# Attention with a routed expert layer: the second half's dense tile becomes the fourth tile of its half, and its keys and values are loaded at other times

## The chip, the cores and the metric

The kernel runs on one core of one Trainium2 chip. A core has TensorE (PE, matmuls and transposes), VectorE (DVE), ScalarE (ACT), GpSimd (POOL) and SyncE (SP, which here issues most of the DMAs). The metric is the device time of one execution in microseconds (us), the median of several runs.

## The reference, cut to what matters

Block-sparse attention over 4 batches, 8 heads, 768 tokens and 24 blocks of 32, then a layer of 8 experts that picks one expert for every token.

```python
mask = np.abs(blk_i - blk_j) <= 1
mask = mask | (blk_i == 0) | (blk_j == 0) | (blk_i == n_blocks - 1) | (blk_j == n_blocks - 1)
for qb in range(n_blocks):
    for kb in sampled_blocks[qb]:                      # 3 sampled blocks
        mask[qb * block:(qb + 1) * block, kb * block:(kb + 1) * block] = True
attn = softmax(np.where(mask, scale * q @ k.T, -1e9))
x = (attn @ v).transpose(0, 2, 1, 3).reshape(B * S, H * D)      # 3072 x 512
logits = x @ w_gate + modality_bias[modality_id]
e_idx = np.argmax(logits, axis=1)
for e in range(E):
    h = np.maximum(x[mask] @ w1[e], 0.0)               # mask = e_idx == e
    out[mask] = gate_w[mask, None] * (h @ w2[e])
```

The first and the last block of queries see all keys ("dense"); the other 22 see a window, the first and the last block and three sampled ones ("sparse").

## The kernel before

The batches are worked off in two halves of two. A half has 12 tiles of 128 tokens (2 batches x 2 blocks x 32): one dense tile (blocks 23 and 0) and 11 sparse ones. The work of a tile is cut into items: a dense tile has eight (`("d", b, pr)`, batch and pair of heads), a sparse tile four (`("s", half, m, n, b)`). The list `items` holds the eight dense items of the first half, then all 88 sparse ones; after the sparse items whose numbers are in `DENSE_AFTER` two dense items of the second half are put in each time.

The loop at the end of attention runs over steps t. In a step, each stage of an item runs `LAG` steps after its first: S scores (L401 dense, L557 sparse), M maxima, X exponentials (L423, L573), T transposes (L433, L582), A copies, W weighted sums (L451 dense, L604 sparse, at lag 7 for dense and 5 for sparse), V the own sampled values (L613, lag 7), O division (L460, L470), Y transposes of the output, G gate. An item's S thus runs at the step that is its index in `items`. Scores are computed for two items at once, at every second step. The order of instructions on every engine is that in which the code is written; each engine works off its own in this order.

Loads hang on steps (`side`). For every sparse tile SyncE issues a query (L146, followed by a load of block numbers into registers, L536), value rows that the tile needs anew (L511 to L517; a half's first two tiles need more of them) and six sampled "own" value blocks (L545), the latter two after the V stage of the tile two before has released their buffer. GpSimd copies a tile's keys together out of the dense keys, which stay in SBUF (`share_k`, L484, L488, L502), and hands on value rows (`share_v`, L527). The dense keys and values of the second half (batches 2 and 3, 1.5 MB each for keys and for values) come in six pieces of 256 KB each (L159 keys, L165 values), every second step from the steps in `DENSE_IN`: values, first half of the keys, second half of the keys. `KD_SLOT` and `VD_SLOT` say which slots of SBUF they take.

A finished tile has a number tau in the order of tokens; two tiles with tau and tau ^ 1 are routed together (`routing`: argmax of the gate, ranks in the expert, L353 and what follows), as "fillers" between the stages. When 16 and 18 tiles are ranked, `choose` picks the experts of the first two groups of 256 tokens, and `rows_of` turns the positions of a group's tokens into the rows to gather (`g_`) and the rows of the output (`s_`); it is called a third time for all other groups. Expert groups gather tokens, split weights into a high and a low part (L752, L755) and run both layers (L810 to L812, L825 to L827); the first two start before attention ends.

Of the kernel before, what the change touches and what calls it, by code (L numbers as in the profile page):

```python
# [15 lines left out]
ALU = mybir.AluOpType  # L16
# [4 lines left out]
P = 128  # L21
B, H, S, D = 4, 8, 768, 64
BLK = 32
# [6 lines left out]
NT = NTOK // P  # L30
# [27 lines left out]
DENSE_DVE = ((0, 0), (0, 1))  # L58
DENSE_AFTER = (21, 29, 45, 47)
LAG = {'d': {'S': 0, 'M': 1, 'X': 2, 'T': 4, 'A': 4, 'W': 7, 'O': 8, 'V': 101, 'Y': 11, 'G': 13}, 's': {'S': 0, 'M': 1, 'X': 2, 'T': 4, 'A': 4, 'W': 5, 'V': 7, 'O': 8, 'Y': 10, 'G': 13}}  # L60
# [13 lines left out]

DENSE_IN = ((19, 14, 30), (49, 38, 44))
Q_IN = 22
# [14 lines left out]
def attention_moe(ctx, tc, kD, qD, qH, v0, v1, blocks, modality, w_gate, bias, w1, w2, out):  # L91
    nc = tc.nc
# [29 lines left out]
    with ExitStack() as actx:  # L122
# [13 lines left out]
        kd, vd = {}, {}  # L136
        KD_SLOT, VD_SLOT = (0, 1, 2, 9), (2, 3, 3, 3)
        ad = slot(4)
# [496 lines left out]
        lgs = {}  # L635

        rank_ends = {4: 0, 8: 4, 12: 8, 14: 12, 16: 14, 18: 16, 20: 18, 22: 20, 24: 22}
        fillers = []
# [416 lines left out]
        def rows_of(tp, n, g_, s_, hold=None):  # L1055
            i_, f_ = ((lambda name, dt=dt: small.tile([P, NCOL], dt, name=name, bufs=1)[:, 0:n]) for dt in (I32, F32))
            pad, tf, to = f_("pad"), f_("tf"), f_("to")
            tk, tb, tn = i_("tk"), i_("tb"), i_("tn")
            nc.vector.tensor_scalar(to, tp[:, 0:n], 0.5, float(NTOK // 2 - 1), ALU.is_lt, ALU.add)
            yield  # L1060
            nc.vector.tensor_tensor(g_, tp[:, 0:n], to, ALU.add)
            if hold is not None:
                ready[NEAR] = True
                while not hold:
                    yield
            yield
            nc.vector.tensor_scalar(pad, tp[:, 0:n], 0.0, 8192.0, ALU.is_equal, ALU.mult)
            nc.vector.tensor_scalar(tk, g_, 7, None, ALU.logical_shift_right)
            yield
            nc.vector.tensor_scalar(tn, g_, 5, 1, ALU.logical_shift_right, ALU.bitwise_and)  # L1070
            nc.vector.tensor_scalar(tf, tk, float(NB // 2), float(-NB // 2), ALU.is_ge, ALU.mult)
            yield
            nc.vector.tensor_scalar(tb, g_, 6, 1, ALU.logical_shift_right, ALU.bitwise_and)
            nc.vector.tensor_tensor(tf, tf, tk, ALU.add)
            yield
            nc.vector.scalar_tensor_tensor(pad, tb, float(S - 2 * BLK), pad, ALU.mult, ALU.add)
            nc.vector.tensor_tensor(to, tf, tn, ALU.add)
            yield
            nc.vector.tensor_scalar(to, to, 0.5, float(S), ALU.is_le, ALU.mult)
            yield  # L1080
            nc.vector.scalar_tensor_tensor(to, tf, float(-2 * BLK), to, ALU.mult, ALU.add)
            yield
            nc.vector.scalar_tensor_tensor(to, g_, float(-BLK), to, ALU.add, ALU.add)
            yield
            nc.vector.tensor_tensor(s_, to, pad, ALU.add)
# [144 lines left out]
        xrs, turns, banks, sums, ats, gated, written = {}, {}, {}, {}, {}, set(), {}  # L1230
# [5 lines left out]
        def tau_of(m, half):  # L1236
            return half * (NT // 2) + m + 1

        def end_tile(m, half):
            tau = tau_of(m, half)  # L1240
            gate(tau, turns.pop((m, half)))
            gated.add(tau)
            if tau ^ 1 in gated:
                t = tau - tau % 2
                fillers.append(routing(t, lgs.pop(t), [xrs.pop((t % (NT // 2) + n - 1, half)) for n in range(2)]))

# [72 lines left out]
        for g in range(2 * NM):  # L1319
            half, m = divmod(g, NM)  # L1320
            t = at["s", half, m, 0, 0]
# [89 lines left out]
        with man:  # L1411
            constants()
            for token in START:
# [3 lines left out]
                elif op == "h":  # L1417
                    t = int(token[1:])
# [90 lines left out]
```

## Time and profile before

| | us |
|---|---|
| median of 3 runs (530.39, 526.32, 525.06) | 526.32 |
| the profiled execution | 523.66 |
| its span | 521.9 |
| PE busy in the span | 499.5 |
| DVE busy | 388.4 |
| ACT busy | 335.5 |
| POOL busy | 244.9 |

Attention fills the span to some 225 us, with the first two expert groups starting in its last part; the other groups follow. Busy times are those of one execution; a busy PE is not PE at its peak.

### The profile page before, as it was taken

The page shows a single profiled execution, that of the slowest core. Times are in us where ns is not written, and L with a number is a line of the kernel's source. Part 1 is how long each engine was busy: PE and PEld are TensorE (multiplying, and loading weights), DVE is VectorE, ACT ScalarE, POOL GpSimd, SP SyncE. Part 2 cuts the span into 40 slices and gives each one's busy share as a digit, 9 for nine tenths or more (in the row PEclk, how much of TensorE's full clock was granted, in tenths as well). Part 3 has the DMA queues.
Part 4 walks back from the last instruction along what each step waited for, and adds up shares of the span by engine and source line. Part 5 has one row for each costly group of instructions (what it writes and reads, how often), then busy time and mean ns, then how long its engine had stood idle before and what let it go on. Part 6 is the DMA issues. An engine that isn't in the chain of part 4 may idle for free.

```text
span 521.9 us, 18958 instructions
## 1 busy us (share of the span) xinstructions
PE 499.5 (96%) x7124; PEld 420.6 (81%) x7124; DVE 388.4 (74%) x1136; ACT 335.5 (64%) x765; POOL 244.9 (47%) x514
## 2 busy tenths in 40 slices
PE   7999999989899999899999999999999999999995
PEld 5667776767778777688989798998989899898974
DVE  5886688686689899967986868667686766768573
ACT  3799787978789978844545655555565545655561
POOL 6779685576458884312275051323324222241423
PEclk9999999999999999999999999999999999999999
DMA  8997885999756778965878797879669696877860
GB/s 293 332 249 227 241 222 184 244 228 258 196 174 191 207 219 245 273 192 200 242 281 294 246 297 258 266 233 301 200 240 284 227 295 202 280 223 251 260 209 25
DMA packets 59063, 123.84 MB, mean 237 GB/s; under 512 B 9681, under 2 KB 17618, under 8 KB 58962
## 3 DMA queue, kind: packets, MB, share of 16 engines
q1 hardware_dynamic: 54704, 108.88, 68.7%
q0 software_dynamic: 4256, 13.65, 7.9%
q8 instruction: 58, 0.95, 0.8%
q14 instruction: 43, 0.35, 0.3%
q10 hardware_dynamic: 2, 0.00, 0.0%
HBM read 105.97 MB, written 12.86 MB: 228 GB/s over the span
## 4 chain that ended last, share of the span: by engine, by line
PE 73%; DMA 11%; DVE 7%; ACT 3%; SPq 2%; issue 2%; POOL 0%; DVEq 0%; POOLq 0%; ACTq 0%
PE bank L810 8%; PE bank L812 8%; PE bank L811 8%; PE bank L827 7%; PE bank L826 7%; PE bank L825 7%; PE bank L557 6%; PE bank L582 6%; DMA slot<-x_d,gi 5%; PE bank L604 3%; PE bank L613 3%; PE bank L451 2%; DMA slot<-w 2%; PE bank L630 2%; PE bank L401 2%
## 5 line engine op out<-in xcount | busy, mean ns | idle before, releaser
L755 DVE TENSOR_TENSOR slot<-slot 128x1024 fp32r<-128x1024 f32 x99 | 124.6, 1272 | 63.1 <-ACT slot L752 54.9
L752 ACT CAST slot<-slot 128x1024 fp32r<-128x1024 f32 x104 | 107.0, 1047 | 68.3 <-PE bank L811 49.5
L810 PE MATMUL bank<-slot 128*128 128x256 f32 x384 | 108.4, 282 | 0.2 <-issue 0.2
L812 PE MATMUL bank<-slot 128*128 128x256 f32 x384 | 107.9, 281 | 0.1
L811 PE MATMUL bank<-slot 128*128 128x256 f32 x384 | 107.6, 280 | 0.0
L573 ACT ACTIVATE a<-y,mn 128x256 f32<-128x256 f32 x176 | 88.7, 511 | 7.9 <-DVE mn L565 7.7
L846 POOL DMA_INDIRECT out<-slot,si x20 | 27.3, 1364 | 109.5 <-ACT slot L842 106.5
L827 PE MATMUL bank<-slot 128*128 128x512 f32 x192 | 75.9, 395 | 0.4 <-DVE slot L818 0.4
L826 PE MATMUL bank<-slot 128*128 128x512 f32 x192 | 75.9, 395 | 0.0
L825 PE MATMUL bank<-slot 128*128 128x512 f32 x192 | 75.8, 395 | 0.0
L810 PEld LDWEIGHTS bank<-slot 128*128 128x128 f32 x384 | 72.3, 188 | 0.6
L811 PEld LDWEIGHTS bank<-slot 128*128 128x128 f32 x384 | 72.2, 188 | 0.6
L812 PEld LDWEIGHTS bank<-slot 128*128 128x128 f32 x384 | 72.2, 188 | 0.3 <-DVE slot L755 0.3
L565 DVE CUSTOM_DVE_ANT_1 y<-bank,smask 128x256 f32<-128x256 f32 x176 | 66.2, 416 | 0.5 <-PE bank L557 0.3
L502 POOL COPY slot<-slot 128x128 f32 x264 | 63.6, 293 | 0.0
L527 POOL TENSOR_SCALAR slot<-slot 32x1024 f32<-32x1024 f32 x40 | 41.7, 1042 | 33.2 <-issue 12.8
L587 ACT COPY at<-bank 128x512 f32<-128x512 f32 x88 | 50.6, 576 | 9.0 <-PE bank L582 9.0
L582 PE MATMUL bank<-ident,a 128*128 128x128 f32 x352 | 52.1, 280 | 3.0 <-issue 2.2
L557 PE MATMUL bank<-slot,q_raw 64*32 64x256 f32 x1408 | 48.7, 382 | 0.0
L582 PEld LDWEIGHTS bank<-ident,a 128*128 128x128 f32 x352 | 38.1, 141 | 7.3 <-issue 2.3
L827 PEld LDWEIGHTS bank<-slot 128*128 128x128 f32 x192 | 36.1, 188 | 9.2 <-DVE slot L818 0.9
L826 PEld LDWEIGHTS bank<-slot 128*128 128x128 f32 x192 | 36.0, 188 | 8.3 <-DVE slot L755 0.4
(307 smaller groups left out, 859.8 us busy)
## 6 DMA issues: line engine op xcount, KB each, us to landing
slot<-w SPq DMA_DIRECT2D x100, 512.0 KB, 5.2
slot<-v SPq DMA_DIRECT2D x180, 128.0 KB, 4.0
x_d<-xr SPq DMA_DIRECT2D x22, 256.5 KB, 4.2
q_raw<-qH SPq DMA_DIRECT2D x22, 256.0 KB, 4.8
slot<-v SPq DMA_DIRECT2D x16, 256.0 KB, 5.1
slot<-slot SPq DMA_DIRECT2D x120, 32.0 KB, 4.4
slot<-kD SPq DMA_DIRECT2D x13, 256.0 KB, 3.6
slot<-v SPq DMA_DIRECT2D x4, 768.0 KB, 12.4
```

What stands on the lines that cost most here:

```text
L557: nc.tensor.matmul(sp[u][32 * pr:32 * pr + 32, b * 256:(b + 1) * 256], lhsT=q[r, b * NPAIR + pr, n, :], rhs=kv[r, s0:s0 + 8, b, pr, :], st ...
L565: nc.vector.tensor_tensor_reduce(y[:, u, :].rearrange("p (s f) -> p s f", s=8), sp[u][:, b * 256:(b + 1) * 256].rearrange("p (s f) -> p s ...
L573: nc.scalar.activation(a[:, u, :], y[:, u, :], AF.Exp, bias=mn[:, u:u + 1], scale=-1.0, accum_out=total[:, u:u + 1])
L582: nc.tensor.transpose(tp[:, k:k + P], a[:, u, c * P:(c + 1) * P], ident)
L752: nc.scalar.copy(h, s)
L755: (eng or (nc.gpsimd if n in POOL_SPLITS else nc.vector)).tensor_tensor(l, s, h.bitcast(F32), ALU.subtract)
L810: nc.tensor.matmul(o, lhsT=h[:, fs], rhs=xh[g % 2][:, c, :], start=c == 0 and f % 2 == 0, stop=False)
L811: nc.tensor.matmul(o, lhsT=h[:, fs], rhs=xl[g % 2][:, c, :], start=False, stop=False)
L812: nc.tensor.matmul(o, lhsT=l[:, fs], rhs=xh[g % 2][:, c, :], start=False, stop=c == 3 and f % 2 == 1)
L825: nc.tensor.matmul(o, lhsT=hh[0][:, f, ts_], rhs=h[:, fs], start=f == 0, stop=False)
L826: nc.tensor.matmul(o, lhsT=hh[0][:, f, ts_], rhs=l[:, fs], start=False, stop=False)
L827: nc.tensor.matmul(o, lhsT=hl[f // 4][:, f % 4, ts_], rhs=h[:, fs], start=False, stop=f == 7)
```

## The change

The dense tile of the second half gets tau 15 instead of 12, the place behind three sparse tiles (`DENSE_PLACE`). Its items go into the list later (`DENSE_AFTER`), its keys earlier and its values later (`DENSE_IN`), and the values of batch 3 go into slot 0 instead of slot 3. `rows_of` takes the new place into account with seven more instructions on VectorE and one `yield` more in each of its three calls. The modality table, which is ordered by tau, is reordered on the host.

```diff
-DENSE_AFTER = (21, 29, 45, 47)
+DENSE_AFTER = (35, 41, 51, 53)
+DENSE_PLACE = (0, 3)
-DENSE_IN = ((19, 14, 30), (49, 38, 44))
+DENSE_IN = ((38, 14, 20), (57, 26, 32))
-        KD_SLOT, VD_SLOT = (0, 1, 2, 9), (2, 3, 3, 3)
+        KD_SLOT, VD_SLOT = (0, 1, 2, 9), (2, 3, 3, 0)
...
             nc.vector.tensor_tensor(tf, tf, tk, ALU.add)
             yield
+            d, first = DENSE_PLACE[1], NT // 2
+            nc.vector.tensor_scalar(dj, tk, float(first), None, ALU.is_ge)
+            yield
+            nc.vector.tensor_scalar(to, tk, float(first + d), float(-d - 1), ALU.is_ge, ALU.mult)
+            nc.vector.tensor_tensor(dj, dj, to, ALU.add)
+            nc.vector.tensor_scalar(to, tk, float(first + d + 1), float(d), ALU.is_ge, ALU.mult)
+            nc.vector.tensor_tensor(dj, dj, to, ALU.add)
             nc.vector.scalar_tensor_tensor(pad, tb, float(S - 2 * BLK), pad, ALU.mult, ALU.add)
             nc.vector.tensor_tensor(to, tf, tn, ALU.add)
+            nc.vector.tensor_tensor(to, to, dj, ALU.add)
             yield
             nc.vector.tensor_scalar(to, to, 0.5, float(S), ALU.is_le, ALU.mult)
             yield
             nc.vector.scalar_tensor_tensor(to, tf, float(-2 * BLK), to, ALU.mult, ALU.add)
+            nc.vector.scalar_tensor_tensor(to, dj, float(2 * BLK), to, ALU.mult, ALU.add)
...
         def tau_of(m, half):
-            return half * (NT // 2) + m + 1
+            return half * (NT // 2) + (DENSE_PLACE[half] if m < 0 else m + (m >= DENSE_PLACE[half]))
+
+        def tile_of(tau):
+            half, n = divmod(tau, NT // 2)
+            return (-1 if n == DENSE_PLACE[half] else n - (n > DENSE_PLACE[half])), half
...
-                fillers.append(routing(t, lgs.pop(t), [xrs.pop((t % (NT // 2) + n - 1, half)) for n in range(2)]))
+                fillers.append(routing(t, lgs.pop(t), [xrs.pop(tile_of(t + n)) for n in range(2)]))
...
-                1, 3, 4, 0, 2)).reshape(P, NT),
+                1, 3, 4, 0, 2).reshape(P, NT)[:, order]),
```

From the table follow these steps. Dense items start at 30, 40, 58 and 62 before, and at 44, 52, 64 and 68 now. Keys of batch 2: 14 to 18 and 30 to 34 before, 14 to 24 now; keys of batch 3: 38 to 48 before, 26 to 36 now. Values of batch 2: 19 to 29 before, 38 to 48 now; of batch 3: 49 to 59 before, 57 to 67 now.

The first place is SyncE's queue at the value loads of the second half's first tile (before, the fifth piece of batch 3's values, an output row, that tile's value rows L511 to L514, a query, the sixth piece):

```order
L165 DMA slot<-v 128x512
L1297 DMA x_d<-xr 128x513
L511 DMA slot<-v 32x1024 x2
L513 DMA slot<-v 32x2x1024
L514 DMA slot<-v 32x2x1024
L146 DMA q_raw<-qH 128x512
L536 TENSOR_LOAD rb_i
L165 DMA slot<-v 128x512
```

After the change (line numbers one higher and more), the same queue at the value rows of the half's second tile, L512 to L518; ahead of this stand the rows of the first tile, the first piece and six own values:

```order
L166 DMA slot<-v 128x512
L147 DMA q_raw<-qH 128x512
L537 TENSOR_LOAD rb_i
L166 DMA slot<-v 128x512
L1311 DMA x_d<-xr 128x513 x2
L512 DMA slot<-v 32x1024 x2
L517 DMA slot<-v 32x1024
L518 DMA slot<-v 32x1024
L166 DMA slot<-v 128x512
```

The six pieces, which before ended at the first tile's value rows, now begin behind them and stand around those of the second tile.

The second place is TensorE where the second half's dense items begin. Before, the scores of its last four come with two sparse items of the half's first tile between them:

```order
L401 MATMUL bank<-slot,qd 64x512 x4
L401 MATMUL bank<-slot,qd 64x256 x4
L597 MATMUL bank<-rexp,fold 32x8 x4
L613 MATMUL bank<-slot,at 32x64 x32
L582 MATMUL bank<-ident,a 128x128 x8
L557 MATMUL bank<-slot,q_raw 32x256 x16
L630 MATMUL bank<-wg_raw,xT 64x8 x8
L604 MATMUL bank<-slot,at 64x64 x16
L582 MATMUL bank<-ident,a 128x128 x4
L620 MATMUL bank<-ident,xr 128x128 x4
L433 MATMUL bank<-ident,a 128x128 x6
L401 MATMUL bank<-slot,qd 64x512 x4
```

Now (L402 dense scores, L558 sparse scores, L434 dense transposes), two tiles further on:

```order
L402 MATMUL bank<-slot,qd 64x512 x4
L402 MATMUL bank<-slot,qd 64x256 x4
L605 MATMUL bank<-slot,at 64x64 x16
L583 MATMUL bank<-ident,a 128x128 x4
L621 MATMUL bank<-ident,xr 128x128 x4
L583 MATMUL bank<-ident,a 128x128 x4
L558 MATMUL bank<-slot,q_raw 32x256 x16
L598 MATMUL bank<-rexp,fold 32x8 x4
L614 MATMUL bank<-slot,at 32x64 x32
L583 MATMUL bank<-ident,a 128x128 x4
L434 MATMUL bank<-ident,a 128x128 x6
L402 MATMUL bank<-slot,qd 64x512 x4
```

The pairs keep their distance of two sparse items and lie beside the same kinds of work, after the half's second tile instead of within its first.

The third place is VectorE in the first call of `rows_of` (before: `to` is the index of the output row, L390 and L565 belong to ranks and attention):

```order
L390 TENSOR_SCALAR lhs<-iota_f,rlo,code 128x128
L1079 TENSOR_SCALAR to<-to 128x2
L1081 SCALAR_TENSOR_TENSOR to<-tf,to 128x2
L458 TENSOR_SCALAR rt<-bank 128x8
L459 RECIPROCAL rt<-rt 128x8
L460 TENSOR_TENSOR xr<-bank,rt 128x512
```

After the change:

```order
L391 TENSOR_SCALAR lhs<-iota_f,rlo,code 128x128
L1080 TENSOR_SCALAR to<-tk 128x2
L1081 TENSOR_TENSOR dj<-dj,to 128x2
L1082 TENSOR_SCALAR to<-tk 128x2
L1083 TENSOR_TENSOR dj<-dj,to 128x2
L1084 SCALAR_TENSOR_TENSOR pad<-tb,pad 128x2
L1085 TENSOR_TENSOR to<-tf,tn 128x2
L1086 TENSOR_TENSOR to<-to,dj 128x2
L1088 TENSOR_SCALAR to<-to 128x2
L459 TENSOR_SCALAR rt<-bank 128x8
L460 RECIPROCAL rt<-rt 128x8
L461 TENSOR_TENSOR xr<-bank,rt 128x512
```

Eight short rows instead of two stand ahead of the division of a tile (L459 to L461).

## Rows read from the trace of the kernel before

**Rows 1.** The page, part 1: busy us, share of the span, instructions.
```profile
PE 499.5 (96%) x7124; PEld 420.6 (81%) x7124; DVE 388.4 (74%) x1136; ACT 335.5 (64%) x765; POOL 244.9 (47%) x514
```

**Rows 2.** Windows of 20 us: length, busy us of each engine, PE clock, DMA share, GB/s.
```profile
40.00:60.00 20.00, 18.88 (x516) 14.50 (x506) 13.56 (x63) 17.40 (x58) 15.66 (x39) 1.00 0.77 227
60.00:80.00 20.00, 19.16 (x466) 14.51 (x464) 15.21 (x70) 16.45 (x54) 15.49 (x47) 1.00 0.84 235
80.00:100.00 20.00, 19.09 (x481) 14.53 (x476) 15.45 (x70) 16.60 (x56) 10.88 (x27) 1.00 0.73 208
100.00:120.00 20.00, 17.45 (x491) 13.78 (x476) 15.37 (x76) 15.22 (x52) 14.64 (x42) 1.00 0.91 237
120.00:140.00 20.00, 18.22 (x423) 13.33 (x423) 13.14 (x56) 16.86 (x54) 7.74 (x25) 1.00 0.94 239
140.00:160.00 20.00, 20.00 (x548) 15.81 (x546) 15.25 (x80) 15.53 (x53) 13.60 (x43) 1.00 0.54 161
...
260.00:280.00 20.00, 20.00 (x125) 17.77 (x125) 18.32 (x36) 10.86 (x14) 11.34 (x8) 1.00 0.81 282
```

**Rows 3.** Timeline of PE, 30 to 200 us: start, us, line, [idle before <- releaser].
```profile
52.36 0.45 PE L604 MATMUL bank<-slot,at 128*64 128x64 f32 x8 [0.81 <-issue]
...
65.48 1.09 PE L557 MATMUL bank<-slot,q_raw 64*32 64x256 f32 x32
...
70.30 1.09 PE L557 MATMUL bank<-slot,q_raw 64*32 64x256 f32 x32
...
71.41 1.23 PE L613 MATMUL bank<-slot,at 128*32 128x64 f32 x64
...
77.21 0.92 PE L451 MATMUL bank<-slot 128*64 128x64 f32 x24 [0.52 <-DVE mn L565]
...
115.47 1.09 PE L582 MATMUL bank<-ident,a 128*128 128x128 f32 x8 [2.18 <-issue]
...
131.40 0.33 PE L433 MATMUL bank<-ident,a 128*128 128x128 f32 x1
133.20 0.70 PE L433 MATMUL bank<-ident,a 128*128 128x128 f32 x5 [1.48 <-issue]
```

**Rows 4.** Timeline of DVE, 109 to 118 us.
```profile
111.95 1.03 DVE L381 CAST rhi<-r 128x4 f32<-128x4 int32 x1
...
114.55 0.69 DVE L460 TENSOR_TENSOR xr<-bank,rt 128x512 f32<-128x512 f32 x1
```

**Rows 5.** Timeline of POOL, 22 to 170 us.
```profile
106.84 2.15 POOL L488 TENSOR_SCALAR slot<-slot 128x256 f32<-128x256 f32 x5 [2.13 <-DMA slot<-kD]
...
111.91 4.40 POOL L527 TENSOR_SCALAR slot<-slot 32x1024 f32<-32x1024 f32 x4
```

**Rows 6.** Windows of 5 us, columns as in rows 2.
```profile
115.00:120.00 5.00, 4.54 (x97) 3.77 (x98) 4.45 (x21) 3.29 (x11) 4.75 (x14) 1.00 1.02 267
...
130.00:135.00 5.00, 3.52 (x115) 2.81 (x114) 3.72 (x10) 3.23 (x11) 2.08 (x2) 1.00 1.01 249
...
200.00:205.00 5.00, 5.00 (x147) 3.60 (x149) 4.80 (x28) 4.58 (x13) 0.42 (x2) 1.00 0.88 259
```

**Rows 7.** Timeline of SP: DMA issues, start, us in the issue.
```profile
96.12 0.86 SPq L146 DMA_DIRECT2D q_raw<-qH  x1
98.49 1.33 SPq L545 DMA_DIRECT2D slot<-v  x3
...
105.91 0.33 SPq L165 DMA_DIRECT2D slot<-v  x1
...
127.33 0.35 SPq L165 DMA_DIRECT2D slot<-v  x1
```

**Rows 8.** DMA issues, 118 to 140 us: count, KB each, median us to landing.
```profile
slot<-v SPq DMA_DIRECT2D x4, 256.0 KB, 6.3
```

**Rows 9.** Two lines of `rows_of`: count, ns min/median/max, first and last start, forms.
```profile
L1059 DVE TENSOR_SCALAR to<-bank x3: 146/156/190, 197.6 to 263.2; 128x2 f32<-128x2 f32 x2, 128x38 f32<-128x38 f32 x1
L1070 DVE TENSOR_SCALAR tn<-gi_e x2: 161/586/1012, 199.2 to 225.3; 128x2 int32<-128x2 int32 x2
```

More of the change, by code (lines that the diff above doesn't have):

```diff
@@ L1056, in rows_of @@
             i_, f_ = ((lambda name, dt=dt: small.tile([P, NCOL], dt, name=name, bufs=1)[:, 0:n]) for dt in (I32, F32))
-            pad, tf, to = f_("pad"), f_("tf"), f_("to")
+            pad, tf, to, dj = f_("pad"), f_("tf"), f_("to"), f_("dj")
             tk, tb, tn = i_("tk"), i_("tb"), i_("tn")
@@ L1486 @@
     k, q = cols(inputs["k"]), cols(inputs["q"])
+    order = [h * (NT // 2) + n for h, d in enumerate(DENSE_PLACE) for n in (*range(1, d + 1), 0, *range(d + 1, NT // 2))]
     arrays = {
```

## The prediction

> **What bounds the kernel now.** I began with the page's busy shares. TensorE is busy 96% of the span [rows 1], so whatever a new order can give back must come out of the 4% in which it waits. The windows of 20 us show where that is in the stretch that the change touches, steps 19 to 72 of the schedule, some 40 to 150 us: from 40 to 140 us TensorE is idle for 1.12, 0.84, 0.91, 2.55 and 1.78 us, 7.20 together [rows 2]. From 140 us to 160 it has no gap, nor has it among the expert groups, the last two rows there [rows 2]. No work of TensorE is removed, so 7.20 us, 1.4% of the span, is the most that a better order here can return.
>
> Then the single waits on TensorE's timeline, four of which hold 4.99 us of the 7.20 [rows 3]. They are of three kinds. At 115.47 it had waited 2.18 us until a transpose could take its PSUM bank: the division of an earlier tile (L460 on VectorE) ended at 115.24 [rows 4], 0.23 us before, and in the program that transpose does wait for VectorE. VectorE was late: a cast of 128x4 took 1.03 us while GpSimd ran four 32x1024 copies back to back for 4.40 us [rows 4, 5], which had piled up behind key copies that waited 2.13 us for a dense key transfer [rows 5]. At 52.36 and 133.20 (0.81 and 1.48 us) TensorE stopped inside a run: of six transposes one started at 131.40 and the other five from 133.20 [rows 3], and the second of them waits for nothing in the program. I take these to be instructions that arrived late, since the queues are full then: DMA share 1.02 at 115 to 120 us and 1.01 at 130 to 135 [rows 6]. At 77.21 (0.52 us) it waits for VectorE behind a pair of dense items.
>
> **The change part by part.** *The order of items.* Nothing is added on TensorE, ScalarE or GpSimd in the attention. The four dense pairs start at steps 44, 52, 64 and 68 instead of 30, 40, 58 and 62. Both routings concerned, of the tile pairs (12, 13) and (14, 15), still become ready at steps 76 and 84, because the last item that each waits for comes as late as before. So from step 84 on all keeps its order, except for the VectorE rows below. The wait behind a dense pair moves with it: 0, with bounds of 0.52 either way.
>
> *The 2.18 us wait.* The last dense keys were issued at step 48, six steps before the key copies that need them; now it is step 36, eighteen before. That takes away GpSimd's wait of 2.13 us, and the two sets of value copies that ran back to back there get these key copies between them (two other sets now stand together, at steps 38 and 42). I count 2.0 of the 2.18 as gained; bounds 0, since VectorE can be late for a bank elsewhere, and 2.18.
>
> *Late instructions.* These waits depend on when a fetch falls into full queues. Four of the six dense value pieces that left in 105 to 122 us go behind that stretch, but there they meet others. I take 0.5 of the 2.29 (0.81 + 1.48) as gained; bounds 2.29 gained and 1.48 lost, one more such wait. The Trainium skill (Runtime: NRT & Kernel Launch, Instruction fetch mechanics) calls the refill of an engine's instructions mostly hidden. By that page these would be ordinary waits that a new order may remove; the gain would be 2.29 and the sum below 1.8 us better. The five transposes that start late without a wait in the program speak against it.
>
> *Values of the third dense batch.* Their last piece was issued at step 29 and needed at step 37; now it is issued at 48 and needed at 51. What there is to spend: from the scores of step 32 (65.48) to the first weighted sum of step 37 (77.21) it is 11.7 us [rows 3], and steps 46 to 51 are built alike; the piece is the sixth of six blocks, some 0.7 us later, so 12.4. What is spent: SyncE is held until the sums of step 46 release a buffer, 2.3 us after that step's scores (70.30 to 71.41 + 1.23 at step 34 [rows 3]); then come two value issues at 0.4 each, a query and a register load (2.37 us from 96.12 to 98.49), three own values (1.33) and its own issue of 0.4 [rows 7]: 7.2 us. A 256 KB value took 6.3 us to land in the busiest stretch [rows 8]: 13.5, so 1.1 us late there, and on time where it lands in 5. I take 0.5; bounds 0 and 2.4 (another set of own values of 1.33 ahead of it).
>
> *Values of the fourth batch.* They went out from 105.91 to 127.33 us [rows 7]; now eight steps later, beside the first loads of the half's first two tiles, which carry more value rows than others, and are needed at step 71. The last piece follows only two values behind the release of step 66: 2.3 + 0.8 + 0.4 + 6.3 = 9.8 us, and the same lead of 12.4 covers it. What is dear is the stretch: four of the six pieces move into it, 4 x 0.262 MB at 249 GB/s [rows 6] is 4.2 us, the upper bound; the queues have room behind it (share 0.54 at 140 to 160 us [rows 2]), the lower bound is 0, and I take 0.3. The Trainium skill (SBUF — State Buffer, Summary: rules for kernel authors) reckons with about 358 GB/s between HBM and SBUF. By that page the queues would not be full at 249, and the 0.3 us would be nothing; the share of 1.01 at 249 GB/s says that they are full.
>
> *Seven more VectorE rows in each of three calls* that turn gathered indices into output rows. Such a row takes 0.15 to 0.16 us undisturbed, and one took 1.01 [rows 9], like the cast beside GpSimd's copies. Two calls lie at 197.6 to 231 us: 14 x 0.155 = 2.2 us. VectorE is busy 4.80 of 5 us there, but TensorE 5.00 [rows 6], so matmuls cover most of it; if that cover is gone, the 2.2 us stand on the path, and 1.7 more if two rows meet a GpSimd copy (0.86 each). I take 0.4; bounds 0 and 3.9. The call has one more step, which makes the second group's choice half a step later; its gather keeps its place among GpSimd's rows: 0. The third call starts at 263.2 us [rows 9], where TensorE is busy 20.00 of 20 [rows 2]: 0, hidden by expert matmuls, and 1.1 if they did not hide it. The slot that now takes the fourth batch's values is last read by key copies issued at step 48, nine steps before the first load: no wait, 0.
>
> Sum: -2.0 - 0.5 + 0 + 0.5 + 0.3 + 0.4 = -1.3 us. The profiled execution took 523.66 us (span 521.9), 2.66 under the median of 526.32, and would come to 522.4; from the median I forecast **525.0 us**.
>
> **The rivals.** *The waits only change place.* VectorE, ScalarE and GpSimd run close behind TensorE in attention; a bank that is free in one place is late in another. For it: the idle time is spread over all five windows. Against it: the largest wait has a chain of its own with the dense keys at its head. Time: 526.3, give or take 1.5.
>
> *All waits of the stretch go.* For it: 140 to 160 us, half empty now, takes over transfers from a full stretch. The gain is 7.20 less the 1.2 of costs, so 520.3. Against it: 2.21 of the 7.20 lies in small waits that no load explains.
>
> *Slower: the fourth batch's values collide with the first tiles of the half.* SyncE then has six pieces, eight value issues of two tiles, twelve own values and two queries in eleven steps. Place: the weighted sum of step 71. It decides once the last piece is issued later than 6.1 us after the scores of step 66 (12.4 less 6.3 to land). Price: the 4.2 us without room, plus one more late fetch of 1.48 while the share stays at 1, and nothing gained: 532.0. Against it: the queues are half empty from 140 us on.
>
> *Slower by the VectorE rows:* 3.9 us on the path less the 2.0 gained, 528.2. It decides where VectorE, at 96%, has no slack left.
>
> **How the numbers follow.** The forecast, a gain of 0 to 4.5 us, gets 0.45; the waits that change place 0.22; all waits gone 0.17; the collision 0.12; the VectorE rows 0.04. A measurement of this kernel can hardly tell less than 1%, 5.3 us, from no change (three runs lay from 525.06 to 530.39). Under 521.1 lies only the case with all waits gone: faster 0.17. Over 531.6 lies only the collision: slower 0.12. Within 1%: 0.71. The range leaves out the collision and a part of the all-gone case (0.2 together), and takes in the VectorE case with the spread of the first rival: 519.5 to 530.0.
>
> **What would show it.** Right: no wait of TensorE over 1 us at the half's first tile; key copies there with no wait for dense keys; DMA share at 140 to 160 us up from 0.54; rows of the new seven near 0.15 us each; the first expert matmuls about 1 us earlier. Wrong: a wait of TensorE at the weighted sums of step 51 or 71 for a value transfer; SyncE issuing value pieces two steps or more behind TensorE; or a gap after 180 us that outweighs it all. I would be most wrong if the stretch from 180 to 240 us, whose order I leave as it is, depended on the phase in which attention reaches it.

## The result, and the profile after

The changed kernel takes 532.29 us (median of six runs, 528.33 to 535.54) against 525.06 for the kernel before (six runs, 523.36 to 530.39): a ratio of 1.0123, 95% interval 1.0086 to 1.016. A second set of runs gave 1.0115 (1.0068 to 1.0162). So it is slower by some 6 us, outside the range given; a gain of 1.3 us was forecast. Executions in which the chip itself ran some per cent slow are left out of all ratios here, and a profile taken of one is not read.

The profiled execution is the slowest of its six (535.54 us, span 533.8), and that has to be kept in mind while reading it. The page's first part, as in [rows 1]:

```profile
PE 507.0 (95%) x7124; PEld 425.0 (80%) x7124; DVE 390.8 (73%) x1157; ACT 336.4 (63%) x765; POOL 247.9 (46%) x514
```

The count of matmuls is the same; VectorE has its 21 rows more. TensorE's busy time has risen by 7.5 us with the same work. The windows of 20 us, columns as in [rows 2]:

```profile
40.00:60.00 20.00, 19.71 (x511) 15.74 (x512) 14.13 (x70) 18.10 (x60) 17.88 (x50) 1.00 0.68 206
60.00:80.00 20.00, 18.59 (x530) 14.22 (x528) 13.63 (x66) 16.44 (x55) 13.08 (x35) 1.00 0.87 247
80.00:100.00 20.00, 18.52 (x436) 13.06 (x434) 12.72 (x56) 14.90 (x47) 13.06 (x35) 1.00 0.86 229
100.00:120.00 20.00, 15.46 (x304) 11.26 (x300) 11.56 (x59) 10.99 (x36) 8.87 (x22) 0.83 0.78 219
120.00:140.00 20.00, 20.00 (x521) 15.53 (x514) 15.28 (x74) 18.36 (x62) 12.48 (x37) 1.00 0.60 176
140.00:160.00 20.00, 19.63 (x450) 14.92 (x458) 15.34 (x64) 16.38 (x52) 11.36 (x32) 1.00 0.87 231
...
220.00:240.00 20.00, 15.37 (x326) 13.84 (x325) 11.71 (x68) 9.67 (x21) 6.40 (x7) 0.83 0.50 140
```

From 120 to 140 us TensorE has no gap now (1.78 us before), and the queues' share has moved from there (0.94 to 0.60) to 140 to 160 us (0.54 to 0.87), as forecast. But two windows are worse than any of before, and in both the granted clock is 0.83. TensorE's timeline says what stands there (line numbers are one higher than before, ten higher behind `rows_of`):

```profile
105.86 0.80 PE L452 MATMUL bank<-slot 128*64 128x64 f32 x20
111.20 0.48 PE L452 MATMUL bank<-slot 128*64 128x64 f32 x4 [4.54 <-DMA slot<-v]
...
112.66 2.84 PE L402 MATMUL bank<-slot,qd 64*64 64x512 f32 x16
...
116.30 1.30 PE L452 MATMUL bank<-slot 128*64 128x64 f32 x24
...
137.36 1.52 PE L402 MATMUL bank<-slot,qd 64*64 64x512 f32 x16
...
227.41 0.78 PE L605 MATMUL bank<-slot,at 128*64 128x64 f32 x20
232.11 0.91 PE L605 MATMUL bank<-slot,at 128*64 128x64 f32 x12 [3.92 <-issue]
```

The first is the weighted sum of step 51: twenty of its 24 matmuls run, then TensorE waits 4.54 us for the sixth block of the third dense batch's values. The second is in the middle of a run of 32 matmuls that wait for nothing in the program; in the kernel before the same run was broken in the same part, for 1.12 us. Behind each of them TensorE runs at its lower level for a while, which the windows of 5 us show:

```profile
110.00:115.00 5.00, 3.80 (x24) 1.82 (x24) 1.96 (x11) 1.68 (x5) 0.00 (x0) 0.54 0.92 233
115.00:120.00 5.00, 5.00 (x92) 3.82 (x84) 2.79 (x11) 1.56 (x3) 0.00 (x0) 0.78 0.46 146
...
230.00:235.00 5.00, 2.89 (x22) 2.77 (x22) 0.23 (x1) 0.63 (x2) 0.00 (x0) 0.50 0.29 103
235.00:240.00 5.00, 5.00 (x109) 4.42 (x108) 4.63 (x31) 3.13 (x5) 1.61 (x2) 0.83 0.07 12
```

Sixteen dense scores take 2.84 us there and 1.52 at 137.36; the 24 matmuls of a weighted sum take 1.30 instead of 0.92 [rows 3]. Between the two profiled executions lie 11.9 us. The two waits make 4.54 + 3.92 - 1.12 = 7.3 of them, and the four windows lack 2.30 + 1.10 + 2.50 + 0.85 = 6.8 us of full clock, at most, since TensorE stood still for a part of them; the vanished waits of 2.18 and 1.48 us [rows 3] go off that. By steps: the scores of step 96 start 5.4 us later than before (201.90 against 196.53), those of step 102 6.9 us later, and the other 5.0 us come behind them.

Why the piece came late stands on SyncE's timeline and on the chain of waits:

```profile
97.06 0.42 SPq L166 DMA_DIRECT2D slot<-v  x1
97.79 1.42 SPq L546 DMA_DIRECT2D slot<-v  x3
99.38 1.24 SPq L166 DMA_DIRECT2D slot<-v  x1
...
102.53 0.35 SPq L147 DMA_DIRECT2D q_raw<-qH  x1
104.40 1.33 SPq L546 DMA_DIRECT2D slot<-v  x3
105.78 0.41 SPq L166 DMA_DIRECT2D slot<-v  x1
```

```profile
105.78 5.38 DMA slot<-v
111.16 0.04 issue
111.20 0.48 PE bank L452 x4
```

The piece left at 105.78, when the sum that needs it had almost begun (105.86). It landed in 5.38 us. What is late is the issue.

### The profile page after: what moved, and what is told of

Read it like the earlier page. It is cut to its first block, busy times and chain, and to the rows that moved or that the text cites. A ratio compares the mean times of both kernels' runs of the same rounds, so it can differ in the third digit from the quotient of the medians.

```text
span 533.8 us, 18974 instructions
## 1 busy us (share of the span) xinstructions
PE 507.0 (95%) x7124; PEld 425.0 (80%) x7124; DVE 390.8 (73%) x1157; ACT 336.4 (63%) x765; POOL 247.9 (46%) x514
## 4 chain that ended last, share of the span: by engine, by line
PE 60%; DVE 15%; DMA 13%; issue 4%; SPq 3%; ACT 3%; POOL 1%; POOLq 0%; DVEq 0%; ACTq 0%
PE bank L811 7%; PE bank L813 7%; PE bank L812 6%; PE bank L827 6%; PE bank L828 6%; PE bank L826 6%; PE bank L558 5%; DMA slot<-x_d,gi 4%; PE bank L583 4%; DMA slot<-v 3%; DVE y L566 3%; PE bank L614 2%; PE bank L605 2%; PE bank L452 2%; DMA slot<-w 2%
## 5 line engine op out<-in xcount | busy, mean ns | idle before, releaser
L756 DVE TENSOR_TENSOR slot<-slot 128x1024 fp32r<-128x1024 f32 x99 | 120.9, 1235 | 60.3 <-ACT slot L753 49.0
L558 PE MATMUL bank<-slot,q_raw 64*32 64x256 f32 x1408 | 50.8, 382 | 0.9 <-issue 0.9
```

What stands on the lines that cost most here:

```text
L558: nc.tensor.matmul(sp[u][32 * pr:32 * pr + 32, b * 256:(b + 1) * 256], lhsT=q[r, b * NPAIR + pr, n, :], rhs=kv[r, s0:s0 + 8, b, pr, :], st ...
L756: (eng or (nc.gpsimd if n in POOL_SPLITS else nc.vector)).tensor_tensor(l, s, h.bitcast(F32), ALU.subtract)
```

## The experiments

Ratios are to the kernel before, run beside the kernel on the same chip, with 95% intervals. "Steps 96 to 102" is read from TensorE's timeline, from the first scores of step 96 to the first of step 102; from there on all orders hold the same matmuls. (The expectations count to the last matmul of scores, 0.7 us more.)

| kernel | ratio | interval | steps 96 to 102, us |
|---|---|---|---|
| before | 1 | | 12.3 |
| changed; again | 1.0123; 1.0115 | 1.0086 to 1.0160; 1.0068 to 1.0162 | 13.8; 14.2 |
| values 3rd batch at 34 to 44 | 1.0067 | 1.0030 to 1.0104 | 14.4 |
| at 39 to 49 | 1.0171 | 1.0112 to 1.0231 | 13.3 |
| at 19 to 29 | 1.0152 | 1.0100 to 1.0205 | 13.8 |
| keys 4th batch at 38 to 48 | 1.0133 | 1.0081 to 1.0186 | 14.1 |
| without the seven rows; again | 1.0078; 1.0079 | 1.0045 to 1.0111; 1.0046 to 1.0113 | 12.0; 12.2 |
| seven rows alone | 1.0040 | 1.0005 to 1.0074 | 13.4 |
| fourteen rows alone | 1.0112 | 1.0058 to 1.0167 | 17.3 |
| five rows on GpSimd | 1.0175 | 1.0125 to 1.0226 | 15.8 |
| new order, old load steps | 1.0104 | 1.0046 to 1.0161 | 15.7 |
| the same without the rows | 1.0046 | 1.0012 to 1.0080 | 12.7 |
| half the new order, no rows | 1.0058 | 1.0019 to 1.0098 | 12.5 |
| changed, rows behind attention; again | 1.0134; 1.0095 | 1.0074 to 1.0194; 1.0058 to 1.0132 | 12.0; not read |
| order and old loads, rows behind | 1.0075 | 1.0042 to 1.0108 | 13.2 |
| before, rows behind; again | 0.9984; 1.0009 | 0.9951 to 1.0017; 0.9970 to 1.0048 | not read; 12.1 |

**The changed kernel again.** No edit.

> The changed kernel once more, beside the runs of the kernel before on one chip, to see which of its waits come back. Theory A (one late piece): the wait at the weighted sum of step 51 is there again, 3 to 5.5 us, with half clock behind it; the time is 1.0 to 1.4% over the kernel before. Theory B (the wait at 228 us, a late fetch of instructions): the wait there comes back at the same matmul, 0.5 to 4 us long, so that its size is chance and the mean loss by it is 1 to 2 us. If the 3.92 us belong to the change, it is over 3 us again.

Its span is 529.2 us, without either of the large waits. TensorE's timeline:

```profile
100.08 0.55 PE L583 MATMUL bank<-ident,a 128*128 128x128 f32 x3 [2.03 <-issue]
...
109.84 0.80 PE L452 MATMUL bank<-slot 128*64 128x64 f32 x20
111.16 0.34 PE L452 MATMUL bank<-slot 128*64 128x64 f32 x4 [0.52 <-DMA slot<-v]
...
210.89 0.64 PE L631 MATMUL bank<-wg_raw,xT 128*64 128x8 f32 x16 [1.67 <-DVE rt L459]
...
227.72 0.57 PE L605 MATMUL bank<-slot,at 128*64 128x64 f32 x12 [0.82 <-issue]
```

and SyncE's:

```profile
105.75 0.43 SPq L166 DMA_DIRECT2D slot<-v  x1
```

The last piece left at the same time, to 0.03 us, and the matmuls that need the block start at the same time (111.16 and 111.20). TensorE only reached them 4 us later, because it had lost those before; 2.03 of them stand at 100.08, inside a run of four transposes. So in these two executions the wait is what is left of a fixed arrival; and since the time over the kernel before is the same, theory A, that one late piece makes the loss, falls with this run. In this profile the scores of step 96 start 4.1 us later than in the kernel before, those of step 102 6.0 us, and only 1.3 us come behind them. The wait at 228 us is 0.82 here, as theory B has it: its size is chance, its place is not.

**When the values are loaded.** One row each (39 and 19 stand for 34 in two more; the last moves the keys of the fourth batch):

```diff
-DENSE_IN = ((38, 14, 20), (57, 26, 32))
+DENSE_IN = ((34, 14, 20), (57, 26, 32))
+DENSE_IN = ((38, 14, 20), (57, 38, 44))
```

> The values of the third dense batch are asked for at steps 34 to 44 instead of 38 to 48, all else as in the changed kernel. Theory A (the late last piece makes the loss): the 4.54 us wait of TensorE at the weighted sum of step 51 and the half clock in the 6.8 us behind it go; 532.3 less 4.5 and some 2.6 is 525.2 us, between 524 and 527. Theory B (the loss lies after 180 us, in a stretch that depends on the phase in which attention reaches it, above all the 3.92 us wait at 228 us): the wait at step 51 goes, but the time stays at 529 or more, or moves by the phase either way. Theory C (the 21 VectorE rows cost it): 529 or more, with the 3.92 us wait still there.

> The values of the third dense batch are asked for one step later still, at steps 39 to 49, all else as in the changed kernel. A step takes some 2.1 us there. Theory A: the wait at the weighted sum of step 51 grows from 4.5 to between 5.6 and 6.8 us, and the time from 532.3 to between 533 and 535. Theory B: the phase behind the wait shifts by 1 to 2 us; the time may go either way by 2 us and the wait at 228 us changes or goes. Theory C: no change, 532.3.

> The changed kernel with the third dense batch's values alone back at the steps of the kernel before, 19 to 29; the keys stay at 14 to 36, the fourth batch's values at 57 to 67. Theory D: the waits for values between 60 and 115 us go, last scores at 208 to 211 us, 0 to 0.4% over the kernel before. Rival O: last scores at 214 us or later, 0.8% or more over. Rival K (what counts is the mass in a stretch, and 20 pieces between 42 and 82 us now fill that one): waits of 2 us or more in 40 to 85 us instead, 0.5 to 1% over.

> The changed kernel with the fourth dense batch's keys at steps 38 to 48, as in the kernel before, and no longer at 26 to 36; the values of the third batch stay at 38 to 48. Theory A: what decides is the last piece's issue, which is as late as before or later by the key issues beside it: a wait of 4.5 to 7 us at the weighted sum of step 51, 1.2 to 1.8% over the kernel before. Theory D: two pieces at each even step, 3.1 MB in the full stretch, so waits for own values beside that one, 1.6 to 2.5% over. If only the count of pieces ahead of step 38 mattered: 1% or less over.

Four steps earlier the wait at step 51 is gone, but in the profile smaller ones stand where it was full, for own values that came behind the dense pieces:

```profile
89.58 1.09 PE L614 MATMUL bank<-slot,at 128*32 128x64 f32 x62 [1.26 <-DMA slot<-v]
...
99.90 1.09 PE L614 MATMUL bank<-slot,at 128*32 128x64 f32 x62 [0.83 <-DMA slot<-v]
...
108.51 1.09 PE L614 MATMUL bank<-slot,at 128*32 128x64 f32 x62 [0.68 <-DMA slot<-v]
```

The profiled execution (535.0 us) is one of the three slowest of its twelve. The time is between the two theories, 0.7% instead of 1.2%, with intervals that overlap. One step later than in the change there are two waits in the same sum, and 0.5% more time:

```profile
107.96 0.34 PE L452 MATMUL bank<-slot 128*64 128x64 f32 x4 [1.50 <-DMA slot<-v]
112.44 0.48 PE L452 MATMUL bank<-slot 128*64 128x64 f32 x4 [4.15 <-DMA slot<-v]
```

At the old steps, 19 to 29, beside keys that now all leave in 14 to 36, it is 1.5% (1.00 to 2.05). Theory D is wrong, and rival K's 0.5 to 1% is exceeded; its waits in 58 to 77 us (0.72, 1.12, 1.81 and 0.57) are shorter than foreseen, and two of them, 0.72 and 1.81, end with no releaser, as does a break of 2.59 us at 105 us. Only rival O's 0.8% or more holds this time. Later keys of the fourth batch bring a wait of 5.06 us at step 51 and 1.3%. That run and the one at 39 to 49 (534.1 us by its ratio to the first 525.06) lie where theory A had them in wait and time; what it cannot hold is the changed kernel's second profile, above, with the loss and without the wait. No place for these loads that was tried gave the whole loss back.

**The VectorE rows.** Without them (left out is the correction of row numbers), alone in the kernel before, twice there, and five of the seven on GpSimd:

```diff
-            nc.vector.tensor_scalar(dj, tk, float(first), None, ALU.is_ge)
...
-            nc.vector.scalar_tensor_tensor(to, dj, float(2 * BLK), to, ALU.mult, ALU.add)
```

```diff
+            nc.vector.tensor_scalar(to, tk, 0.0, 0.0, ALU.is_ge, ALU.mult)
+            for _ in range(6):
+                nc.vector.tensor_tensor(dj, dj, to, ALU.add)
```

```diff
-            nc.vector.tensor_scalar(dj, tk, float(first), None, ALU.is_ge)
+            nc.gpsimd.tensor_scalar(dj, tk, float(first), None, ALU.is_ge)
...
```

> The changed kernel without the seven added VectorE rows and without the added step in each of the three calls that turn gathered indices into output rows; left out is the correction of the row numbers for the second half's dense tile, so rows of the output stand in other places. Theory A: the wait of 4.5 us at step 51 stays and the time is 531 to 533. Theory B: the wait at 228 us stays within 1 us of its place, 531 to 533. Theory C: the time falls to 526 to 529 and the wait at 228 us goes.

> The kernel before with only the seven added VectorE rows and the added step in each of the three calls; order of items, times of the dense loads and buffers as before. Theory A and theory B: 525.1 to 526, no more than 0.9 us over the kernel before. Theory C: 527 to 530, with a new wait of TensorE over 1 us between 220 and 235 us.

> The kernel before with twelve added VectorE rows and one step in each call (the first five of the change, and seven that add zero), and the two last of the change: fourteen in all. Order and loads as before. Theory R: twice the cost of the seven, steps 96 to 103 at 15 to 16 us instead of 13.0 before and 14.1 with seven, 0.6 to 1.0% over the kernel before. If the seven cost nothing by themselves: 0.4% or less.

> The changed kernel with five of the seven rows of each call on GpSimd, which is busy 6 of 13 us in steps 96 to 103; two stay on VectorE. Nothing is left out. Theory R: those steps fall from 14.5 to 15.0 us towards 13.3, and the time from some 1.15% over the kernel before to 0.7 to 0.9%. If the rows' cost is the length of their chain and not VectorE's time: no gain, 1.1% or more, since a row on GpSimd is slower and adds two changes of engine.

Seven rows cost 0.40% alone (0.05 to 0.74), and the change without them is 0.36 to 0.45% faster than with them: some 2 us both ways. Fourteen cost 1.1% (0.58 to 1.67). Where it happens, VectorE's timeline of the changed kernel's second profile shows, in steps 96 to 102:

```profile
205.34 0.16 DVE L382 CAST rhi<-r 128x2 f32<-128x2 int32 x1
...
205.63 0.16 DVE L1078 TENSOR_SCALAR dj<-tk 128x2 f32<-128x2 int32 x1
205.70 1.22 DVE L756 TENSOR_TENSOR slot<-slot 128x1024 fp32r<-128x1024 f32 x1
...
207.78 0.16 DVE L1080 TENSOR_SCALAR to<-tk 128x2 f32<-128x2 int32 x1
207.97 0.16 DVE L1081 TENSOR_TENSOR dj<-dj,to 128x2 f32<-128x2 f32 x1
208.17 1.02 DVE L1082 TENSOR_SCALAR to<-tk 128x2 f32<-128x2 int32 x1
209.22 0.16 DVE L1083 TENSOR_TENSOR dj<-dj,to 128x2 f32<-128x2 f32 x1
209.30 1.00 DVE L1084 SCALAR_TENSOR_TENSOR pad<-tb,pad 128x2 f32<-128x2 int32 x1
210.22 0.15 DVE L1085 TENSOR_TENSOR to<-tf,tn 128x2 f32<-128x2 f32 x1
210.41 0.16 DVE L1086 TENSOR_TENSOR to<-to,dj 128x2 f32<-128x2 f32 x1
...
210.68 0.16 DVE L459 TENSOR_SCALAR rt<-bank 128x8 f32<-128x8 f32 x1
```

and that of the kernel before, the same two ends:

```profile
201.43 0.16 DVE L381 CAST rhi<-r 128x2 f32<-128x2 int32 x1
...
204.30 0.16 DVE L458 TENSOR_SCALAR rt<-bank 128x8 f32<-128x8 f32 x1
```

From the cast to the division's first row it was 2.87 us and is now 5.34. The division frees a bank, and TensorE waits for it at 210.89 (1.67 us, above). Of the seven new rows six stand in between, five of 0.16 us and one of 1.02 (L1082). L1084, 1.00 us here, is a row that the kernel before had too, where it took 0.16; the added step has put it behind the new ones. Both long rows run while GpSimd copies (from 208.11 for 2.18 us), and they make 1.7 of the 2.47 us. With fourteen rows the same matmul waits longer:

```profile
210.98 0.64 PE L631 MATMUL bank<-wg_raw,xT 128*64 128x8 f32 x16 [2.91 <-DVE rt L459]
```

On GpSimd the rows take 0.20 to 0.25 us each, but the first waits 6.29 us for VectorE, and the copies that TensorE needs stand behind it; the change is slower by another half per cent:

```profile
201.39 0.23 POOL L1079 TENSOR_SCALAR dj<-tk 128x2 f32<-128x2 int32 x1 [6.29 <-DVE tk L1069]
...
210.54 1.15 PE L605 MATMUL bank<-slot,at 128*64 128x64 f32 x32 [2.05 <-POOL slot L528]
```

**The order alone.** The new order with the old load steps, with and without the rows; and only the first two pairs moved (this one also with the old load steps and without the rows):

```diff
-DENSE_IN = ((38, 14, 20), (57, 26, 32))
+DENSE_IN = ((19, 14, 30), (49, 38, 44))
```

```diff
-DENSE_AFTER = (35, 41, 51, 53)
+DENSE_AFTER = (35, 41, 45, 47)
```

> The new order of items, the new buffer for the fourth batch's values and the VectorE rows, but every dense load at the steps of the kernel before (values from steps 19 and 49, keys from 14, 30, 38 and 44). Theory D (1.57 MB of values put into the stretch from 75 to 115 us, whose queues are full, make whatever transfer is needed soonest late): no wait over 1.5 us for a value between 60 and 120 us, last scores of attention at 209 to 211 us in the profile, and 0 to 0.4% over the kernel before. Rival O (the order itself: sixteen sparse steps in a row without a dense pair ask for own values faster than the queues bring them): waits for own values between 70 and 115 us stay, last scores at 214 us or later, 0.8% or more over the kernel before.

> The new order of items and the new buffer, every dense load at the steps of the kernel before, and none of the seven VectorE rows (the row numbers lack the correction for the second half's dense tile, so output rows stand in other places). Theory R (the rows cost some 2 us, since VectorE bounds the last eight steps of attention and reaches into the experts; the order itself costs nothing): steps 96 to 103 take 12.5 to 13.2 us as in the kernel before, and the time is within 0.3% of it. Rival O (the order itself costs): 0.6% or more over the kernel before, with the loss ahead of step 84.

> The changed kernel without the seven rows once more (the same left out as before), beside the last one on one chip: the two differ in the steps of the dense loads alone. Theory D (late values in the full stretch cost 2 to 4 us): 0.4 to 0.8% over the order without moved loads, the difference ahead of step 84. If the loads cost nothing: the same time within 0.3%.

> As order_no_rows (no added rows, old load steps, the row numbers without their correction), but only the first two dense pairs stand later, at steps 44 and 52; the last two stay behind the same sparse items as in the kernel before. If the first two pairs cost it: 0.35 to 0.6% over the kernel before. If the last two do: 0 to 0.2% over. If both halves do: 0.2 to 0.35%.

The order itself costs 0.46% (0.12 to 0.80), which neither theory R nor D had; the moved loads cost the rest up to 0.79%, measured beside it on the same chip, 0.33%, and that difference is not larger than its uncertainty. Rival O's time is met with the rows (1.04%, where it asked for 0.8 or more) and missed without them (0.46, where it asked for 0.6). Its mechanism is not there: with the old loads no wait for own values from 70 to 115 us is over 0.3 us (the largest wait of TensorE for a transfer anywhere from 40 to 240 us is 0.45 us without the rows). With half the order moved it is 0.58%, so the first two pairs seem to carry it; the interval (0.19 to 0.98) does not exclude that both do.

**The rows behind attention.** The indices that the gather needs come as before; what only the scattering needs is run after the last item:

```diff
-            yield from rows_of(tp, 2, gi_e[i], si_e[i])
+            yield from rows_of(tp, 2, gi_e[i], si_e[i], late=late_rows)
...
+                    while len(given) < len(late_rows):
+                        given.append(True)
+                        choosers.append(late_rows[len(given) - 1])
```

> The changed kernel with the rows of the first two calls that only the scattering of results needs (nineteen a call, the seven among them) put behind attention; the gather's indices come as before. Nothing is left out. Theory R (the rows stand on VectorE ahead of the divisions that TensorE waits for in steps 96 to 103): those steps take 12 to 13.2 us instead of 14.5 to 15.0, and the time falls from 1.15% over the kernel before to 0.4 to 0.8%. If what counts is the number of rows wherever they stand: no change, 1.0 to 1.3%, the loss now between the last gate and the experts.

> The kernel before with the twelve rows a call that only the scattering needs put behind attention. Theory R: VectorE bounds steps 96 to 103 in it too, so they fall from 13.0 to 11.5 to 12.5 us and the time by 0.1 to 0.4%. If TensorE had caught up there already: the same within 0.1%.

> The new order with all dense loads at the steps of the kernel before, and the nineteen rows behind attention as in after_late. If the order itself costs nothing: 0.1% under to 0.2% over the kernel before. If it costs the 0.46% that it did without the rows: 0.2 to 0.6% over, and the loss stands ahead of step 84. If moved loads cost nothing: the same as after_late.

> The changed kernel with nineteen rows a call behind attention, once more. Theory R (place on VectorE): 0.6 to 0.9% over the kernel before, like the kernel without the seven rows. Theory N (the number of rows counts wherever they stand): 1.1 to 1.3% over.

> The kernel before with twelve rows a call behind attention, once more. Theory R: 0.1 to 0.3% under the kernel before. Theory N: the same within 0.1%.

Steps 96 to 102 come down as theory R says, in the changed kernel from 13.8 and 14.2 us to 12.0. The time does not follow: 1.34 and 0.95% against 1.23 and 1.15 before the edit, where theory R had 0.4 to 0.8 and then 0.6 to 0.9. With the old load steps it is 0.75%, above the 0.2 to 0.6 that the order's own cost would give. The kernel before with its own twelve rows moved is at 0.9984 and 1.0009, no gain that can be told, and no version here beats it. So the stretch is shortened by what was said, but the time of the whole shows no gain from it; where it is lost is not shown. Of the versions that reach the end of attention soon, two show a longer break in the run of weighted sums there: 2.73 us with the order and the late rows, 3.19 in the kernel before with late rows, against 1.12 before; a third shows none over 0.5. That is too uneven to call it the cause.

## Why the prediction was wrong, point by point

**The sum.** It was -2.0 - 0.5 + 0 + 0.5 + 0.3 + 0.4 = -1.3 us. By the experiments, with 1% as 5.3 us: the order with its waits +2.4 (I had -2.5), the two terms of values together +1.7 (I had 0.8), the VectorE rows +2.1 (I had 0.4); together +6.2, which is the change as measured (1.15 to 1.23%). The intervals of the first and last are 1.8 us either way, that of the loads 2.5. The split also depends on the way taken: with the rows in place the moved loads cost 0.11% (1.0115 against 1.0104), with the rows behind attention 0.59 (1.0134 against 1.0075), and on the new order with the old loads the rows cost 0.58. Only the sum is firm.

**The 2.18 us wait and the late instructions.** This is the step that failed: 2.5 us of gain were booked here, and the runs show none. As forecast, GpSimd waits for no dense key any more, and neither the 2.18 nor the 1.48 us are in the profile after; from 120 to 195 us the largest wait is 0.16 us there (0.92 in the second profile). But the reading on which 2.0 of the 2.5 us rested was wrong. VectorE's division did not hold that transpose. In the kernel before with its rows moved behind attention (second set), which has the same work up to there, the same transpose starts before that division has ended (115.66):

```profile
114.97 0.69 DVE L460 TENSOR_TENSOR xr<-bank,rt 128x512 f32<-128x512 f32 x1
...
115.38 1.09 PE L582 MATMUL bank<-ident,a 128*128 128x128 f32 x8 [1.91 <-issue]
```

With the seven and the fourteen rows alone it starts 0.93 and 0.67 us after that end, and not 0.23. It is the same transpose in all four profiles with the order of before, 1.63 to 2.18 us late, also where GpSimd waits for a dense key for 3.72 to 4.85 us instead of 2.13. What such waits share is another thing. The page of the kernel before lists, among the DMA queues, one of kind "instruction" (packets, MB, share):

```profile
q8 instruction: 58, 0.95, 0.8%
```

I took its packets, of 16 KB each, one by one from the 18 profiles read here. Between 40 and 260 us TensorE has 81 waits of 0.5 us or more that end with no releaser, and every one of them ends 1.1 to 1.8 us after such a packet has landed; the 68 waits that end with a releaser lie anywhere from 0.03 to 6.2 us behind one. By this timing, which no run varied on purpose, the 2.18 us are late instructions like the 1.48, and earlier dense keys could not buy them off. With the new order a break of this kind stands at another transpose, the second of four in step 46: 2.03 us at 100.08 in the changed kernel's second profile, above, and 2.03, 1.75, 2.03 and 3.12 us in the four other profiles with the loads of the change. Only the first profile has none, and that one waited 4.54 us for the values.

So I booked the vanished waits as gains and let nothing come back, and as much came back. From the scores of step 20 to those of step 84, the same work in either order, TensorE is idle for 7.20 us in the kernel before (4.33 to 7.27 in the three others of that order), for 8.09 and 6.58 in the changed kernel's two profiles, and for 5.94 to 7.25 in the four others with its loads. My first rival, the waits that only change place, described it, though not the time of the whole.

Why the order without moved loads and rows is still 2.4 us slower could not be found: the profiled execution of the kernel without the rows is the second fastest of its twelve (526.26 of 526.22 to 532.63 us), so the loss of the median is not in its trace. The scores of step 96, ahead of the new rows, start at 195.3 to 198.8 us in the four profiles with the order and loads of before, at 195.0 to 198.6 in the three with the new order and the old loads (202.5 with half the order moved), and at 196.9 to 201.9 in the six with the moved loads, 2 us later in the mean: in the traces the loads cost something there, and the order alone nothing that can be told from the spread. Its 2.4 us stay open. In the profile with the order alone and no rows it is not the stretch 180 to 240 us by the phase either, which I named as my worst case: steps 96 to 102 take 12.7 us and what follows is as before. For the median this is not shown.

The late instructions are a tax on every kernel here. Waits of TensorE that end with no releaser, these among them, sum up to 7.35 us between 40 and 260 us in the kernel before and to between 4.4 and 11.6 in the seventeen other profiles; with the new order and the old loads it is 6.0 to 8.6, so the order pays neither more nor less. The break in the run of weighted sums near 228 us came back in all profiles but one, behind its 17th to 21st matmul, for 0.55 to 3.92 us. The page of the Trainium skill weighed in the prediction (Runtime: NRT & Kernel Launch, Instruction fetch mechanics) has the refill mostly hidden. The traces agree for most of the packets, some 40 in that stretch, but in the mean 4.5 a profile end a wait of 0.5 us or more.

**Values of the third dense batch.** The mechanism stood in the prediction, and also the place: the sum of step 51. I estimated 1.1 us late and took 0.5. Six profiles with these load steps show 4.54, 0.52, 1.35, 1.34, 1.15 and none: 1.25 in the median. What was off is a part of the working. The landing took 5.38 us where I had 6.3, and the lead was 12.2 us (94.49, the scores of step 46, to 106.66) where I had 12.4. But the piece left 11.3 us after those scores (10.1 to 10.5 in the five other profiles) and not 7.2: I counted the issues of two steps from a row in which SyncE was up to date, while it was already behind from the pieces and own values before. Ahead of the piece, its rows of three own values take up to 2.05 us instead of 1.33, and the piece before it took 1.24 us to issue.

**Values of the fourth batch.** Right in the place: the largest wait for them at step 71 is 0.52 us, in one profile, and none in the changed kernel's own two; DMA share at 140 to 160 us up from 0.54 to 0.87, and no collision. No run moves these loads alone, so the 0.3 us are not measured by themselves. The slower rival, to which I gave 0.12, had the sign and nearly the time (532.0) by luck: the collision that it priced is not there.

**The VectorE rows.** The rows take 0.15 to 0.2 us, as forecast, and two rows beside GpSimd's copies 1.0, one of them not new, as the bound said. The term was mis-sized, 0.4 for 2.1, because I took TensorE's busy share of 200 to 205 us, 5.00 of 5 [rows 6], for cover. The window of 20 us from 200 to 220 in the same trace has VectorE busy for 19.27 us:

```profile
200.00:220.00 20.00, 18.23 (x486) 14.23 (x486) 19.27 (x96) 17.37 (x49) 6.48 (x7) 1.00 0.90 255
```

VectorE did not hold TensorE there yet (it is idle for 0.07 us in steps 96 to 102, and the one longer wait behind them, 1.24 us at 214.99, is for ScalarE), but it had 0.73 us left for rows of 2.2 us and more. With the rows TensorE waits for VectorE, for 1.67 us at 210.89 in the changed kernel's second profile. The bound of 3.9 us held it. Whether it is the place of the rows or their number that costs was put to the test twice, and the answer is not clean: the place decides how long that stretch is, and the time of the whole does not follow it. This stays open too.

## What to carry to other kernels

A wait that is taken away where engines run close behind each other is a gain only if the next thing to be late is known; book the sum of a stretch's idle time, not the wait. What ends a wait is read from more than one execution: a release that stands 0.23 us ahead of the end in one trace may stand 0.93 us ahead, or behind, in the next. The lead of a load is counted from the issue queue's own timeline in the stretch it moves to, with its backlog, not from a queue that is up to date. An engine is not covered because another is busy: small instructions on it are free only where it has time to spare or nothing that is waited for stands behind them in its queue.

## What was not expected of the hardware

A wait of TensorE can cost more than its length. Behind the 4.54 us wait and behind the 3.92 the granted clock is about half, the level of 1.2 GHz, and then full again; after waits of 1.5 to 2.6 us it fell in some profiles and not in others (after 2.03 us it did in one and did not in two others; after the 2.18 of the kernel before it did not). The mean granted clock is 0.989 over the twelve runs of the changed kernel and 0.994 over 102 of the kernel before; of some 530 us these are 5.9 and 3.3 us of full clock that are missing, some 2.6 of the 5.6 us between the two means.

Also, two executions of one kernel differ by 7 us in their two largest waits alone, while the last piece leaves SyncE at the same time to 0.03 us, 105.75 (at 103.62 to 105.88 in the four other kernels with these load steps). One profile of the changed kernel suggested a cause for all of the loss, and the next showed the loss without it.
